# New due times for the planner of a channel-attention and rational-FFN kernel, and a new price for its accumulating transfers

## The chip, the cores and the metric

The kernel runs on one core of a Trainium2 chip. The metric is the device time of one execution in microseconds. The kernel before took 2661.84 us, the median of 3 runs (2660.5 to 2662.58).

## The reference, cut to what matters

There are B = 4 batches of N = 6080 rows with C = 256 channels. Attention runs over channels, so its score matrix is 256 x 256 and each batch needs all of its q and k before the first output row can be made:

```python
qn = q / (norm(q, axis=1) + 1e-6); kn = k / (norm(k, axis=1) + 1e-6)
s = kn.transpose(0, 2, 1) @ qn / tau        # 256 x 256 per batch
a = softmax(s);  x = v @ a                  # 24320 rows of 256
h = x @ w_in                                # 256 -> 2048
P = a0 + a1*h + a2*h*h + a3*h*h*h
Q = 1 + |b0|*|h| + |b1|*h*h
out = (P / (Q + 1e-6)) @ w_out              # 2048 -> 256
```

## The kernel before, in words

**Tiling.** Each batch is cut into 12 groups of 512 rows (the last has 448). The softmax of a batch is folded into w_in (method `fuse`, line 734), so a group is v times eight fused weight tiles and then the rational function. Eight pairs of 128 of the 2048 columns make up a group. In `pair` (line 824) PE writes the pair's h into the two banks of a PSUM tile hx (`mm1`), ACT, DVE and POOL work out P/Q with tiles d, r, uu, gh and gl, and PE multiplies the result by w_out into the one tile acc (`mm2`). There are three hx tiles. `finish_pe` (line 1023) copies acc out by ACT, turns it on PE (the rows acc<-ident,orow), copies it again and stores it. Each pair has one of a few recipes: `KIND` has a four-letter word for each of the eight, and its second letter (F or U here) picks the form of the denominator.

**Attention of the next batch.** `Attn.half` (line 563) runs once for each of the 24 half groups of a batch. It loads k and q (tile kq, four slots), multiplies them on PE (rows hx<-kq, and acc<-kq for the first 12 halves of batch 1, which sum in the acc tile before group 0 gets it), squares them on ACT into one of two sq tiles, and adds the squares to the tile ssq by an accumulating DMA issued from POOL. Each such DMA waits for the one before, since both write ssq. `softmax` (line 621) takes ssq for the norms and then makes the fused weights w.

**The order.** No engine takes its order from the program text. Every operation is handed to `step` with an engine, a cost in us and a due time, and `Planner.order` plays them through once, on the host, while the kernel is built: whenever a modelled engine is free it takes the ready operation with the smallest due time, if its buffers have free slots. A due time is a rank and not a release: an operation due far ahead is taken when nothing due earlier is ready. Some tags hand out their slots in rank order as well. The operations are then emitted in the modelled order, and each engine's queue on the chip is bound to it. So a price that is wrong in the model puts an operation into a queue at a place where the chip must wait. `HOP` is what a result takes in the model to reach another engine; for SP it is 3.5 us, which stands for a transfer.

The due time of a pair's operation is the pair's start, 6.5 us (`II`) a pair, plus `LAG[name][p]`; those of everything else come from `TIME`. Times in `TIME` for attention count in units of 6.5 us from the first group of the batch before (`attn` the pace of the halves, `attn0` where they begin, `attn1` the softmax; `attn_0` and `attn0_0` are the same for batch 1, `front` and `front_pace` for its first 12 halves in us). `start` is where group 0 stands.

**The accumulating transfer in the model.** It is a POOL step of 1.0 us that issues it, followed by an SP step of 0.1 us that runs nothing on the chip and only holds the buffers until the transfer may be taken for landed.

Of the kernel before, what the change touches and what calls it, by code (L numbers as in the profile page):

```python
# [13 lines left out]
AF = mybir.ActivationFunctionType  # L14
ALU = mybir.AluOpType
# [3 lines left out]


LAG = {
    "first": (28.264, 1.351, 30.596, -31.998, 48.265, -7.633, 5.766, 9.407),
    "second": (69.447, 11.924, 13.488, 14.684, 30.047, 41.519, -36.921, -20.262),
    "line": (29.753, 17.275, 56.929, -8.355, -26.962, 38.298, 21.628, 26.132),
    "prod": (-0.029, 21.467, 10.987, 11.927, -9.36, -1.03, 19.608, 29.168),
    "abs": (-26.316, 13.409, 15.158, 16.407, 9.682, 24.255, 8.14, 35.331),
    "one": (96.579, 50.039, 85.796, 127.919, 69.732, 205.132, 99.577, 137.256),
    "slope": (45.923, 29.066, -3.324, 65.5, 12.412, 33.873, 79.042, 20.039),
    "num1": (96.685, 110.5, 60.471, 49.954, 94.518, 84.321, 49.923, 91.338),
    "num2": (2.399, -34.469, -46.621, -37.114, -74.499, -79.273, -83.368, -70.543),  # L30
    "sum": (6.768, -18.247, -28.557, 47.285, -22.402, 24.35, -8.822, -10.898),
    "root": (8.242, 1.503, -31.737, 10.696, -14.224, 31.999, -6.895, -29.514),
    "square": (-59.868, -74.162, -39.607, -12.799, -53.597, -105.617, -43.626, -28.859),
    "quot": (31.717, 37.625, 15.75, 23.688, 20.407, 54.6, 28.307, 47.483),
    "again": (-142.994, -152.496, -145.689, -152.346, -180.413, -123.122, -130.534, -108.094),
    "rest": (-93.002, -56.099, -0.318, -35.317, -0.702, -42.223, -38.726, -56.991),
    "last": (-38.743, -19.238, -20.621, 5.667, -11.108, 14.73, 19.5, -28.157),
    "last_pool": (44.147, 41.875, 61.645, 13.609, 34.415, 42.425, 14.139, -6.356),
    "out": (-5.88, 17.18, 22.743, 26.545, 22.215, 34.239, 21.815, 21.52),
    "out_lo": (90.27, 83.799, 51.937, 68.774, 58.601, 126.426, 69.023, 46.848),  # L40
}
TIME = {
    "pair": 6.5, "start": 100.961, "load": 1.875, "softmax": 71.531, "in": 4.844,
    "late_in": -75.156, "out0": -60.692, "out": 7.965, "attn0_0": -9.298, "attn_0": 1.066,
    "attn0": 72.774, "attn": 0.868, "attn1": 92.735, "value": -3.227, "fuse": 4.772,
    "back": 2.637, "store": -9.728, "finish": -20.927, "front": 41.688, "front_pace": 6.569,
    "ahead_pe": 550004.933, "ahead_act": 339878495500000.0, "ahead_dve": 1357688625.0, "ahead_pool": 12442972510.0,
}


# [231 lines left out]
def tile_channel_attention_rational_ffn(  # L282
# [145 lines left out]
        dve.scalar_tensor_tensor(broot[:, 2:3], broot[:, 2:3], 0.5, broot[:, 1:2], op0=ALU.mult, op1=ALU.mult)  # L428
        dve.tensor_tensor(b1r, broot[:, 0:1], broot[:, 2:3], op=ALU.add)

    if any(kind[1] == "G" for kind in KIND):
        square_root()
    w_in_sb = const.tile([P, NC2, F], F32, name="w_in_sb")
    count = {"R": 0, "S": 0}
# [106 lines left out]
    class Attn:  # L541
# [21 lines left out]
        def half(self, i, at, both, sps):  # L563


            g, half = divmod(i, 2)
            base, pn = groups[g]
            first = self.b == 0
            home = "r" if first and i % 6 >= 3 else "kq"
            kq = buf(home, [P, T // 2, 2, C], F32, "kq")  # L570

            def load():
                for j, src in ((0, k), (1, q)):
                    rows = src[self.b, base : base + pn * T].rearrange("(p t) c -> p t c", t=T)
                    sp.dma_start(kq[:pn, :, j, :], rows[:, half * T // 2 : (half + 1) * T // 2, :])

            step("SP", 1.6, at - (0 if first else 3 if i < self.front else 2 * II), load, self.gate, [kq])

            self.kq[half] = kq
            if first or i < self.front:  # L580
                fn = lambda: self.products(sps, [kq], pn, i == 0, i == (self.front or 2 * NG) - 1)
                step("PE", 1.75, both, fn, [kq, sps] if i else [kq], [sps])
                if i == self.front - 1:
                    fn = lambda: dve.tensor_copy(self.sacc.tile, sps[:, :512])
                    step("DVE", 0.66, both + 1, fn, [sps], [self.sacc])
            elif half == 1:
                pair, slot = list(self.kq), bank("hA")
                step("PE", 3.5, both, lambda: self.products(slot, pair, pn, True, True), pair, [slot])
                if i == 1:
                    fn = lambda: dve.tensor_copy(self.sacc.tile, slot.tile)  # L590
                    step("DVE", 0.66, both + 1, fn, [slot], [self.sacc])
                else:
                    fn = lambda: dve.tensor_tensor(self.sacc.tile, slot.tile, self.sacc.tile, op=ALU.add)
                    step("DVE", 0.66, both + 1, fn, [slot, self.sacc], [self.sacc])
            src = kq, lambda: kq[:pn].rearrange("p t j c -> p (t j c)")
            if i == 0:
                sq = self.ssq = buf("orow" if first else "ssq", [P, 2 * 2 * C], F32)
                step("ACT", 1.05, at, lambda: act.activation(sq[:pn], src[1](), AF.Square), [kq], [sq])
            else:
                sq, total = buf("sq", [P, 2 * 2 * C], F32), self.ssq  # L600
                step("ACT", 1.05, at, lambda: act.activation(sq[:pn], src[1](), AF.Square), [kq], [sq])
                own = first and i % 4 == 3
                e = dve if own else pool
                fn = lambda: e.tensor_tensor(total[:pn], sq[:pn], total[:pn], op=ALU.add)
                if SSQ == "DMA" and not first:
                    begun = Buf()
                    fn = lambda: pool.dma_start(total[:pn], sq[:pn], accum_op=ALU.add)
                    step("POOL", 1.0, at + 2, fn, [sq, total], [begun])
                    step("SP", 0.1, at + 2, lambda: None, [begun, sq, total], [total])
                else:  # L610
                    step(*(("DVE", 1.2) if own else ("POOL", 2.38)), at + 2, fn, [sq, total], [total], True)

# [211 lines left out]
    def pair(m, at, vparts, w, acc):  # L824
# [10 lines left out]
        def c(b):  # L835
            return b[:, :, :n]
# [30 lines left out]
        if kind[1] in "Ff":  # L867
            fn = lambda: act.activation(c(kk), c(hx), AF.Abs, scale=b1)
            put("ACT", 0.87, 0.25, "first", fn, [hx], [kk], 1.0)
            fn = lambda: dve.scalar_tensor_tensor(c(d), c(kk), b0, c(hx), op0=ALU.add, op1=ALU.mult)  # L870
            put("DVE", 1.06, 0.22, "prod", fn, [kk, hx], [d], 1.0)
            fn = lambda: act.activation(c(d), c(d), AF.Abs)
            put("ACT", 0.87, 0.2, "abs", fn, [d], [d])
        elif kind[1] == "G":
            fn = lambda: act.activation(c(d), c(hx), AF.Square, scale=b1r)
            put("ACT", 0.87, 0.25, "first", fn, [hx], [d], 1.0)
            fn = lambda: act.activation(c(kk), c(hx), AF.Abs, scale=b0)
            put("ACT", 0.87, 0.25, "second", fn, [hx], [kk], 1.0)
            fn = lambda: dve.scalar_tensor_tensor(c(d), c(kk), ONE, c(d), op0=ALU.add, op1=ALU.add)
            put("DVE", 1.06, 0.22, "prod", fn, [kk, d], [d], None, True)  # L880
        else:
            fn = lambda: act.activation(c(d), c(hx), AF.Square)
            put("ACT", 0.87, 0.16, "first", fn, [hx], [d], 1.0)
            fn = lambda: act.activation(c(kk), c(hx), AF.Abs, scale=b0)
            put("ACT", 0.87, 0.25, "second", fn, [hx], [kk], 1.0)
            if kind[1] == "A":
                fn = lambda: act.activation(c(d), c(d), AF.Identity, scale=b1, bias=ONE)
                put("ACT", 0.87, 0.27, "line", fn, [d], [d])
            else:
                fn = lambda: pool.tensor_scalar(c(d), c(d), b1, ONE, op0=ALU.mult, op1=ALU.add)  # L890
                put("POOL", 1.06, 0.07, "line", fn, [d], [d])
            fn = lambda: pool.tensor_tensor(c(d), c(d), c(kk), op=ALU.add)
            put("POOL", 2.32, 0.06, "sum", fn, [d, kk], [d])
# [4 lines left out]
        put("DVE", 1.06, 0.16, "num1", fn, [y, hx], [y])  # L898
        fn = lambda: dve.scalar_tensor_tensor(c(hx), c(y), a1, c(hx), op0=ALU.add, op1=ALU.mult)
        put("DVE", 1.06, 0.23, "num2", fn, [y, hx], [hx])  # L900
        fn = lambda: act.activation(c(r), c(d), AF.Abs_reciprocal_sqrt, bias=ONE if kind[1] in "Ff" else 0.0)
        put("ACT", 0.87, 0.2, "root", fn, [d], [r], 6.0)
        if kind[1] == "F":
            fn = lambda: pool.tensor_scalar(c(d), c(d), ones[:, 0:1], ONE, op0=ALU.mult, op1=ALU.add)
            put("POOL", 1.06, 0.07, "one", fn, [d], [d])
        elif kind[1] == "f":
# [212 lines left out]
```

## Time and profile before

| | us |
|---|---|
| median of 3 runs | 2661.84 |
| the profiled execution, its own time | 2666.34 |
| its span, first to last instruction | 2664.3 |
| PE busy | 2555.0 (96%) |
| DVE busy | 2463.1 (92%) |
| POOL busy | 2301.2 (86%) |
| ACT busy | 2235.7 (84%) |

PE is the matmul engine, PEld its weight loads (beside PE), DVE the vector engine, ACT the scalar engine, POOL is GpSimd and SP the engine that issues loads and stores. Nearly every row has line 68, because one helper (`InOrder`) records all operations, so rows are told apart by their tiles: out<-in, without buffer numbers.

### The profile page before, as it was taken

The numbers are of one execution on the slowest core, as the hardware profiler recorded it, in microseconds if no ns is written. First come the engines' busy times: TensorE is split into PE (matmuls) and PEld (weight loads), VectorE is DVE, ScalarE is ACT, GpSimd is POOL, SyncE is SP. The second block draws the span as 40 slices with busy tenths as digits, with TensorE's granted clock in tenths as the row PEclk, the third lists the DMA queues.
The fourth block names the chain that finished last, engine by engine and source line by source line (L and its number), as shares of the span: only waits on it lengthen the run. The fifth ranks groups of instructions, "written<-read, shape, count | busy, mean of one in ns | idle before, by whom it ended". The sixth has DMA issues, their size and how long they took to land.

```text
span 2664.3 us, 30195 instructions
## 1 busy us (share of the span) xinstructions
PE 2555.0 (96%) x9920; PEld 1829.5 (69%) x9920; DVE 2463.1 (92%) x2911; ACT 2235.7 (84%) x2287; POOL 2301.2 (86%) x1773
## 2 busy tenths in 40 slices
PE   7799999999999999999999999999999999999998
PEld 6577766666666666667777666666777766666665
DVE  7689999999979999998888999999787999999997
ACT  5588888888878888988878889888886888888986
POOL 6298999999868999998877999999885899999997
PEclk9899999999999999999999999999999999999999
DMA  9954001001120110105741110101671110110100
GB/s 312 223 131 79 16 16 32 17 15 32 32 55 16 28 21 16 32 16 127 174 91 39 25 24 16 31 18 24 150 172 30 23 25 16 28 21 17 23 9 15
DMA packets 290493, 145.76 MB, mean 55 GB/s; under 512 B 205568, under 2 KB 278528, under 8 KB 290336
## 3 DMA queue, kind: packets, MB, share of 16 engines
q1 hardware_dynamic: 280496, 108.04, 17.2%
q0 software_dynamic: 9840, 35.79, 7.5%
q8 instruction: 78, 1.28, 0.2%
q14 instruction: 79, 0.65, 0.1%
HBM read 83.10 MB, written 24.90 MB: 41 GB/s over the span
## 4 chain that ended last, share of the span: by engine, by line
PE 44%; DVE 27%; ACT 8%; DMA 8%; issue 7%; POOL 5%; SPq 0%; DVEq 0%; POOLq 0%; ACTq 0%
PE hx L68 24%; PE acc L68 20%; DVE d L68 9%; DVE hx L68 8%; DVE uu L68 6%; DMA ssq<-sq 5%; ACT uu L68 4%; POOL d L68 4%; DVE gh L68 2%; ACT r L68 2%; DMA kq<-in_q_dram 2%; DVE orow L68 1%; ACT d L68 1%; POOL gl L68 1%; DMA r<-in_q_dram 1%
## 5 line engine op out<-in xcount | busy, mean ns | idle before, releaser
L68 PE MATMUL hx<-vhi,w 128*128 128x512 f32 (+1 forms) x3072 | 1109.2, 415 | 54.4 <-DVE d L68 37.9
L68 PEld LDWEIGHTS hx<-vhi,w 128*128 128x128 f32 x3072 | 580.9, 189 | 270.9 <-DVE d L68 71.6
L68 PE MATMUL acc<-uu,w_out_sb 128*128 128x512 f32 (+1 forms) x1536 | 690.8, 589 | 1.9 <-DVE uu L68 1.9
L68 PE MATMUL hx<-vlo,w 128*128 128x512 f32 (+1 forms) x1536 | 600.6, 391 | 0.0
L68 POOL TENSOR_TENSOR gl<-d,r 128x512 fp32r<-128x512 f32 (+1 forms) x384 | 497.8, 1312 | 65.5 <-DVE d L68 23.7
L68 POOL TENSOR_TENSOR d<-d,gh 128x512 f32<-128x512 f32 (+1 forms) x384 | 486.2, 1287 | 52.1 <-DVE gh L68 45.2
L68 POOL TENSOR_TENSOR d<-d,r 128x512 f32<-128x512 f32 (+1 forms) x384 | 488.2, 1301 | 31.1 <-ACT r L68 30.2
L68 ACT ACTIVATE uu<-hx,babs 128x1024 f32<-128x1024 f32 (+1 forms) x384 | 422.3, 1100 | 97.6 <-PE hx L68 97.5
L68 DVE SCALAR_TENSOR_TENSOR hx<-uu,coef,hx 128x1024 f32<-128x1024 f32 (+1 forms) x384 | 485.5, 1271 | 2.5
L68 ACT ACTIVATE r<-d 128x1024 f32<-128x1024 f32 (+1 forms) x384 | 401.6, 1047 | 98.9 <-POOL d L68 93.8
L68 PEld LDWEIGHTS acc<-uu,w_out_sb 128*128 128x128 f32 x1536 | 291.2, 190 | 278.9 <-issue 259.3
L68 DVE TENSOR_TENSOR uu<-uu,hx 128x1024 f32<-128x1024 f32 (+1 forms) x384 | 458.7, 1201 | 9.6 <-ACT uu L68 9.5
L68 ACT ACTIVATE uu<-hx,coef 128x1024 f32<-128x1024 f32 (+1 forms) x384 | 457.7, 1192 | 2.8 <-DVE d L68 2.8
L68 ACT ACTIVATE r<-r 128x1024 f32<-128x1024 f32 (+1 forms) x384 | 400.9, 1045 | 5.0
L68 DVE SCALAR_TENSOR_TENSOR d<-uu,babs,hx 128x1024 f32<-128x1024 f32 (+1 forms) x288 | 364.0, 1264 | 33.0 <-ACT uu L68 29.9
L68 POOL TENSOR_SCALAR d<-d,ones 128x1024 f32<-128x1024 f32 (+1 forms) x288 | 326.2, 1135 | 49.5 <-ACT r L68 49.2
L68 ACT ACTIVATE d<-d 128x1024 f32<-128x1024 f32 (+1 forms) x288 | 301.6, 1048 | 70.6 <-DVE d L68 70.2
L68 PEld LDWEIGHTS hx<-vlo,w 128*128 128x128 f32 x1536 | 291.1, 190 | 76.8 <-issue 31.2
L68 DVE SCALAR_TENSOR_TENSOR hx<-hx,coef,r 128x512 f32<-128x512 f32 (+1 forms) x384 | 287.8, 750 | 30.1 <-ACT r L68 23.2
L68 DVE SCALAR_TENSOR_TENSOR d<-hx,coef,d 128x512 f32<-128x512 f32 (+1 forms) x384 | 279.9, 738 | 15.3 <-POOL d L68 15.1
L68 DVE SCALAR_TENSOR_TENSOR gh<-hx,coef,r 128x512 fp32r<-128x512 f32 (+1 forms) x384 | 274.7, 737 | 17.3 <-ACT r L68 10.8
L68 DVE SCALAR_TENSOR_TENSOR uu<-d,hx 128x512 f32<-128x512 f32 (+2 forms) x392 | 261.5, 677 | 20.7 <-POOL d L68 9.2
(99 smaller groups left out, 2893.6 us busy)
## 6 DMA issues: line engine op xcount, KB each, us to landing
ssq<-sq POOLq DMA_DIRECT2D x63, 512.0 KB, 5.7
out_dram<-orow SPq DMA_DIRECT2D x184, 128.0 KB, 2.4
vst<-in_v_dram SPq DMA_DIRECT2D x176, 128.0 KB, 3.8
kq<-in_k_dram SPq DMA_DIRECT2D x78, 256.0 KB, 4.3
kq<-in_q_dram SPq DMA_DIRECT2D x78, 256.0 KB, 5.1
d<-in_moe_w_in_dram SPq DMA_DIRECT2D x8, 512.0 KB, 7.0
ssq<-sq POOLq DMA_DIRECT2D x6, 448.0 KB, 5.4
r<-in_k_dram SPq DMA_DIRECT2D x10, 256.0 KB, 6.5
```

What stands on the lines that cost most here:

```text
L68: ins = op(*args, **kwargs)
```

## The change

Every number of `LAG` and nearly every number of `TIME` is another one. The accumulating transfer's two steps in `Attn.half` get other costs and the SP step another due time. A branch for two new second letters of `KIND`, M and m, is added to `pair`; `KIND` itself is the same.

```diff
-    "first": (28.264, 1.351, 30.596, -31.998, 48.265, -7.633, 5.766, 9.407),
+    "first": (71.3429, 5.5381, 15.3656, 17.3995, 31.0379, -4.663, 41.4562, 27.4064),
-    "slope": (45.923, 29.066, -3.324, 65.5, 12.412, 33.873, 79.042, 20.039),
+    "slope": (-10.955, -25.1691, -21.2353, 3.0526, 3.2465, 29.9361, 19.4443, -40.1467),
-    "out": (-5.88, 17.18, 22.743, 26.545, 22.215, 34.239, 21.815, 21.52),
+    "out": (28.5433, 38.827, 36.0652, 56.0077, -1.6481, 39.3464, 48.688, 25.9075),
...
-    "pair": 6.5, "start": 100.961, "load": 1.875, "softmax": 71.531, "in": 4.844,
-    "late_in": -75.156, "out0": -60.692, "out": 7.965, "attn0_0": -9.298, "attn_0": 1.066,
-    "attn0": 72.774, "attn": 0.868, "attn1": 92.735, "value": -3.227, "fuse": 4.772,
-    "back": 2.637, "store": -9.728, "finish": -20.927, "front": 41.688, "front_pace": 6.569,
+    "pair": 6.5, "start": 119.6723, "load": 1.9885, "softmax": 85.1688, "in": 4.4825,
+    "late_in": -65.9811, "out0": -65.8034, "out": 8.3068, "attn0_0": -2.9056, "attn_0": 1.1935,
+    "attn0": 6.2283, "attn": 1.1347, "attn1": 92.9936, "value": 5.1431, "fuse": 5.8883,
+    "back": 5.3039, "store": -112.0259, "finish": -11.5937, "front": 38.819, "front_pace": 9.8779,
...
-    if any(kind[1] == "G" for kind in KIND):
+    if any(kind[1] in "GMm" for kind in KIND):
...
                     fn = lambda: pool.dma_start(total[:pn], sq[:pn], accum_op=ALU.add)
-                    step("POOL", 1.0, at + 2, fn, [sq, total], [begun])
-                    step("SP", 0.1, at + 2, lambda: None, [begun, sq, total], [total])
+                    step("POOL", 0.95, at + 2, fn, [sq, total], [begun])
+                    step("SP", 2.0, at - 50.0, lambda: None, [begun, sq, total], [total])
...
+        elif kind[1] in "Mm":
...
-        if kind[1] == "F":
+        if kind[1] in "Fm":
```

## Rows read from the trace of the kernel before

**Rows 1.** The page: span, busy time of each engine, and the chain.
```profile
span 2664.3 us, 30195 instructions
...
PE 2555.0 (96%) x9920; PEld 1829.5 (69%) x9920; DVE 2463.1 (92%) x2911; ACT 2235.7 (84%) x2287; POOL 2301.2 (86%) x1773
...
PE 44%; DVE 27%; ACT 8%; DMA 8%; issue 7%; POOL 5%; SPq 0%; DVEq 0%; POOLq 0%; ACTq 0%
...
by line: PE hx L68 24.1%; PE acc L68 19.5%; DVE d L68 8.6%; DVE hx L68 8.4%; issue 6.9%; DVE uu L68 6.4%; DMA ssq<-sq 5.3%; ACT uu L68 4.3%; POOL d L68 3.6%; DVE gh L68 1.9%; ACT r L68 1.6%; DMA kq<-in_q_dram 1.5%; DVE orow L68 1.3%; ACT d 
```

**Rows 2.** Busy time of each engine in ten stretches: us, each engine's, clock, DMA.
```profile
0.00:200.00 200.00, 165.98 (x662) 128.16 (x663) 154.18 (x222) 131.81 (x152) 122.27 (x91) 0.95 0.87 222
200.00:254.70 54.70, 54.70 (x213) 39.39 (x212) 48.99 (x56) 47.15 (x47) 48.80 (x40) 1.00 0.43 76
254.70:694.50 439.80, 431.54 (x1651) 301.37 (x1649) 431.62 (x491) 387.72 (x384) 411.52 (x313) 1.00 0.12 22
694.50:874.40 179.90, 165.30 (x633) 118.37 (x634) 158.70 (x199) 144.93 (x162) 136.98 (x109) 0.96 0.18 38
874.40:1222.80 348.40, 342.25 (x1312) 239.51 (x1311) 341.25 (x390) 306.05 (x302) 327.33 (x248) 1.00 0.12 25
1222.80:1426.70 203.90, 195.32 (x803) 149.20 (x802) 165.29 (x210) 162.25 (x179) 154.00 (x128) 0.98 0.58 128
1426.70:1872.80 446.10, 438.08 (x1679) 307.04 (x1678) 436.50 (x498) 392.29 (x388) 416.07 (x315) 1.00 0.13 25
1872.80:2076.80 204.00, 195.06 (x803) 149.58 (x802) 165.60 (x209) 159.59 (x176) 152.36 (x126) 0.98 0.52 113
2076.80:2616.70 539.90, 530.09 (x2032) 371.08 (x2031) 529.01 (x605) 476.77 (x472) 502.32 (x382) 1.00 0.10 20
2616.70:2664.30 47.60, 36.66 (x145) 25.84 (x143) 31.93 (x42) 27.12 (x31) 29.53 (x27) 0.94 0.09 21
```

**Rows 3.** PE in order of time: start, us, what, idle before and what ended it.
```profile
547.97 1.04 PE L68 MATMUL acc<-ident,orow 128*128 128x128 f32 x8
...
597.60 1.04 PE L68 MATMUL acc<-ident,orow 128*128 128x128 f32 x8
...
972.54 1.04 PE L68 MATMUL acc<-ident,orow 128*128 128x128 f32 x8
...
989.72 0.50 PE L68 MATMUL hx<-vhi,w 128*128 128x512 f32 x1 [0.22 <-DVE uu L68]
...
1020.26 0.50 PE L68 MATMUL hx<-vhi,w 128*128 128x512 f32 x1 [0.85 <-DVE d L68]
...
1021.76 1.03 PE L68 MATMUL acc<-ident,orow 128*128 128x128 f32 x8
```

**Rows 4.** Busy time, in Rows 2's columns, of four single groups.
```profile
972.50:1021.80 49.30, 48.24 (x186) 33.66 (x185) 48.51 (x56) 43.78 (x44) 46.30 (x36) 1.00 0.12 22
254.70:302.70 48.00, 48.00 (x185) 33.58 (x184) 47.16 (x54) 41.94 (x42) 44.25 (x34) 1.00 0.12 23
302.70:350.80 48.10, 46.90 (x179) 32.51 (x178) 47.23 (x54) 43.01 (x43) 44.51 (x35) 1.00 0.11 23
820.30:874.40 54.10, 50.04 (x185) 34.52 (x186) 51.07 (x58) 45.72 (x46) 45.78 (x36) 0.97 0.11 20
```

**Rows 5.** Waits of the whole span: who for whom, us in total, times, longest.
```profile
POOL ssq L68 <- DMA ssq<-sq: 49.8, 23, 8.2
...
PE hx L68 <- DVE d L68: 38.5, 39, 4.3
...
PE hx L68 <- DVE uu L68: 16.2, 36, 3.3
```

**Rows 6.** Waits of the first 200 us, and POOL in order of time there.
```profile
POOL ssq L68 <- DMA ssq<-sq: 31.3, 8, 8.2
...
92.73 0.85 POOL L68 DMA_DIRECT2D ssq<-sq  x1 [7.54 <-DMA ssq<-sq]
101.77 0.85 POOL L68 DMA_DIRECT2D ssq<-sq  x1 [8.20 <-DMA ssq<-sq]
...
116.79 0.86 POOL L68 DMA_DIRECT2D ssq<-sq  x1 [5.72 <-DMA ssq<-sq]
```

**Rows 7.** POOL in order of time at the first change of batch.
```profile
742.16 0.91 POOL L68 DMA_DIRECT2D ssq<-sq  x1 [7.01 <-ACT sq L68]
747.26 0.86 POOL L68 DMA_DIRECT2D ssq<-sq  x1 [4.18 <-DMA ssq<-sq]
755.54 1.12 POOL L68 TENSOR_SCALAR d<-d,babs 128x1024 f32<-128x1024 f32 x1 [7.42 <-ACT d L68]
```

**Rows 8.** POOL's waits from 1180 to 2080 us.
```profile
POOL ssq L68 <- DMA ssq<-sq: 14.3, 14, 2.0
```

**Rows 9.** The page's issues and groups: transfers into ssq, PE's score products.
```profile
ssq<-sq POOLq DMA_DIRECT2D x63, 512.0 KB, 5.7
...
L68 POOL DMA_DIRECT2D ssq<-sq x69 | 63.2, 916 | 80.3 <-DMA ssq<-sq 49.8 <-ACT sq L68 10.3 <-ACT kq L68 8.6
...
L68 PE MATMUL hx<-kq 128*128 128x256 f32 (+1 forms) x576 | 134.3, 387 | 13.5 <-DMA kq<-in_q_dram 8.2 <-DVE uu L68 4.8 <-DVE d L68 0.5
```

**Rows 10.** Tile ssq in the first 260 us: its transfers.
```profile
L68 POOL DMA_DIRECT2D ssq<-sq x23: 828/877/1145, 61.1 to 228.3; - x23
...
DMA to landing us min/median/max: 4.5/5.8/8.5
```

**Rows 11.** PE in order of time after the first change of batch.
```profile
848.48 0.61 PE L68 MATMUL acc<-gl,w_out_hi 128*128 128x512 f32 x2
852.39 0.50 PE L68 MATMUL hx<-vhi,w 128*128 128x512 f32 x1 [3.29 <-DVE uu L68]
```

**Rows 12.** PE in order of time before group 0's first output matmul.
```profile
105.04 3.44 PE L68 MATMUL acc<-kq 128*128 128x256 f32 x8 [2.17 <-DMA kq<-in_q_dram]
...
117.78 1.97 PE L68 MATMUL acc<-kq 128*128 128x256 f32 x8 [0.62 <-DMA kq<-in_q_dram]
...
124.00 1.99 PE L68 MATMUL acc<-kq 128*128 128x256 f32 x8 [0.43 <-DMA kq<-in_q_dram]
...
128.97 0.73 PE L68 MATMUL acc<-gh,w_out_hi 128*128 128x512 f32 x2 [0.21 <-DVE gh L68]
```

More of the change, by code (lines that the diff above doesn't have):

```diff
@@ L21 @@
 LAG = {
-    "first": (28.264, 1.351, 30.596, -31.998, 48.265, -7.633, 5.766, 9.407),
[L23 to L27, printed above, removed]
-    "slope": (45.923, 29.066, -3.324, 65.5, 12.412, 33.873, 79.042, 20.039),
@@ L29 @@
[L29 to L35, printed above, removed]
@@ L36 @@
-    "rest": (-93.002, -56.099, -0.318, -35.317, -0.702, -42.223, -38.726, -56.991),
-    "last": (-38.743, -19.238, -20.621, 5.667, -11.108, 14.73, 19.5, -28.157),
-    "last_pool": (44.147, 41.875, 61.645, 13.609, 34.415, 42.425, 14.139, -6.356),
-    "out": (-5.88, 17.18, 22.743, 26.545, 22.215, 34.239, 21.815, 21.52),
-    "out_lo": (90.27, 83.799, 51.937, 68.774, 58.601, 126.426, 69.023, 46.848),
+    "first": (71.3429, 5.5381, 15.3656, 17.3995, 31.0379, -4.663, 41.4562, 27.4064),
+    "second": (57.6016, 6.8299, -20.0392, 65.122, 96.9876, 47.321, 68.033, 47.1333),
@@ new lines @@
+    "line": (65.7742, 85.1844, 45.4807, 69.7028, 102.0524, 52.2186, 86.2735, 119.3282),
+    "prod": (33.6481, -7.9932, 4.2523, 42.8326, 18.6723, 16.8824, -2.3377, 19.7801),
+    "abs": (-71.6274, -40.8391, -65.9086, -29.463, -32.4482, -52.5393, -46.5113, -29.7792),
+    "one": (118.6179, 105.7, 117.0345, 203.3396, 130.0145, 100.6619, 145.5188, 77.3421),
+    "slope": (-10.955, -25.1691, -21.2353, 3.0526, 3.2465, 29.9361, 19.4443, -40.1467),
+    "num1": (78.6651, 58.3606, 83.6887, 98.6281, 88.3287, 36.9504, 89.5643, 90.0089),
@@ new lines @@
+    "num2": (46.2571, 80.0602, 16.4088, 11.9094, -1.0456, 4.5931, 59.9879, 61.4115),
+    "sum": (123.5526, 77.3211, 81.9855, 64.5573, 78.7551, 62.6624, 184.172, 113.5227),
+    "root": (-28.4521, 11.318, -8.4956, 16.0516, -31.2587, -31.8165, -45.0896, -6.9328),
+    "square": (-14.8172, -36.2736, -35.4794, -76.1768, -62.6297, -97.7208, -140.174, -40.3461),
+    "quot": (55.2294, 25.4683, 30.8856, 87.5384, 92.8464, 97.6642, 90.6668, 50.555),
+    "again": (-156.4485, -135.3792, -114.9349, -150.0496, -110.0526, -129.5206, -172.006, -114.8621),
@@ L41 @@
+    "rest": (3.3676, -65.6467, -68.3869, -44.3422, 10.847, -31.6385, 17.7613, -49.8193),
+    "last": (-31.2746, -86.867, 3.8763, 4.0279, -58.0312, -35.3341, -67.6828, 2.1951),
+    "last_pool": (37.4081, 42.1254, -1.8947, 86.973, 138.0179, 64.0258, 43.4222, 50.4234),
+    "out": (28.5433, 38.827, 36.0652, 56.0077, -1.6481, 39.3464, 48.688, 25.9075),
+    "out_lo": (47.5891, 37.4739, 55.257, 34.8831, 115.3163, 109.322, 93.1246, 39.3377),
 }
 TIME = {
-    "pair": 6.5, "start": 100.961, "load": 1.875, "softmax": 71.531, "in": 4.844,
@@ L44 @@
-    "late_in": -75.156, "out0": -60.692, "out": 7.965, "attn0_0": -9.298, "attn_0": 1.066,
-    "attn0": 72.774, "attn": 0.868, "attn1": 92.735, "value": -3.227, "fuse": 4.772,
-    "back": 2.637, "store": -9.728, "finish": -20.927, "front": 41.688, "front_pace": 6.569,
-    "ahead_pe": 550004.933, "ahead_act": 339878495500000.0, "ahead_dve": 1357688625.0, "ahead_pool": 12442972510.0,
+    "pair": 6.5, "start": 119.6723, "load": 1.9885, "softmax": 85.1688, "in": 4.4825,
+    "late_in": -65.9811, "out0": -65.8034, "out": 8.3068, "attn0_0": -2.9056, "attn_0": 1.1935,
@@ L48 @@
+    "attn0": 6.2283, "attn": 1.1347, "attn1": 92.9936, "value": 5.1431, "fuse": 5.8883,
+    "back": 5.3039, "store": -112.0259, "finish": -11.5937, "front": 38.819, "front_pace": 9.8779,
+    "ahead_pe": 93600.5434, "ahead_act": 7.669400039e+16, "ahead_dve": 15227466580.0, "ahead_pool": 4964001.483,
 }
@@ L873, in pair @@
             put("ACT", 0.87, 0.2, "abs", fn, [d], [d])
+        elif kind[1] in "Mm":
+            fn = lambda: act.activation(c(d), c(hx), AF.Square, scale=b1r)
+            put("ACT", 0.87, 0.25, "first", fn, [hx], [d], 1.0)
+            fn = lambda: act.activation(c(kk), c(hx), AF.Abs, scale=b0)
+            put("ACT", 0.87, 0.25, "second", fn, [hx], [kk], 1.0)
+            if kind[1] == "M":
+                fn = lambda: act.activation(c(d), c(d), AF.Identity, bias=ONE)
+                put("ACT", 0.87, 0.2, "line", fn, [d], [d])
+            begun = Buf()
+            fn = lambda: pool.dma_start(c(d), c(kk), accum_op=ALU.add)
+            put("POOL", 0.0, 0.95, "sum", fn, [d, kk], [begun])
+            step("SP", 2.0, at + LAG["sum"][p] - 50.0, lambda: None, [begun, d, kk], [d])
         elif kind[1] == "G":
@@ L900, in pair @@
         put("DVE", 1.06, 0.23, "num2", fn, [y, hx], [hx])
-        fn = lambda: act.activation(c(r), c(d), AF.Abs_reciprocal_sqrt, bias=ONE if kind[1] in "Ff" else 0.0)
+        fn = lambda: act.activation(c(r), c(d), AF.Abs_reciprocal_sqrt, bias=ONE if kind[1] in "Ffm" else 0.0)
         put("ACT", 0.87, 0.2, "root", fn, [d], [r], 6.0)
-        if kind[1] == "F":
+        if kind[1] in "Fm":
             fn = lambda: pool.tensor_scalar(c(d), c(d), ones[:, 0:1], ONE, op0=ALU.mult, op1=ALU.add)
```

## The prediction

> **What bounds the kernel now.** I read the page's totals first, then cut the span into ten stretches at the points where a group's output is turned on PE (the rows acc<-ident,orow), then the waits of each stretch, and last the single stalls. In the totals PE is busy 2555.0 of 2664.3 us and DVE 2463.1 [rows 1]. The change removes no instruction, so PE's work stays and what can be won is PE's idle time: 2664.3 - 2555.0 = 109.3 us, 4.1%. The ten stretches say where it lies, as length minus PE busy [rows 2]: 34.0 before 200 us, 0 to 254.7, 8.3 to 694.5, 14.6 to 874.4, 6.1 to 1222.8, 8.6 to 1426.7, 8.0 to 1872.8, 8.9 to 2076.8, 9.8 to 2616.7, 10.9 in the tail; together 109.3. Three kinds are to be seen. The front (34.0) waits for loads and for the first softmax. Three short stretches hold a change of batch (14.6, 8.6, 8.9); in the second and third of them the next batch's score products run too. The four long ones are steady groups: 9 + 7 + 9 + 11 = 36 periods with 32.2 us idle, 0.9 each.
>
> One steady period is 1021.76 - 972.54 = 49.22 us from turn to turn [rows 3]. In it PE idles 1.06 us and DVE is busy 48.51 of 49.30; the group from 254.7 does the same matmuls in 48.0 us with PE never idle, beside a DVE that has 47.16 to do there [rows 4]. So in a steady group PE and DVE are both nearly full; the idle microsecond is mostly PE's wait for a bank of hx that DVE still reads, as 0.85 us at 1020.26 [rows 3], and over the run PE's matmuls into hx wait 38.5 us for DVE d and 16.2 for DVE uu [rows 5]. Which instruction is late there is a matter of order, and the order is what changes.
>
> The chain of waits gives 5.3% (141 us) to DMA ssq<-sq [rows 1]. That is not what the transfers cost: the chain follows one thread, while PE is busy through most of these pieces. POOL itself waits 49.8 us for them in 23 waits [rows 5]: 31.3 in the first 200 us [rows 6], 4.2 in the first change of batch [rows 7], 14.3 in the other two [rows 8].
>
> **The change part by part.** (1) What does not run. No entry of KIND has M or m as its second letter (they are F and U), and none has G, so the new branch, the two wider tests and the square root leave the program as it was: 0.
>
> (2) The planner's price of an accumulating transfer. Its POOL part goes from 1.0 to 0.95 (the rows have a mean of 916 ns [rows 9]), and its empty SP step from 0.1 to 2.0 us; with SP's 3.5 us of hand-over the planner now sees the sum of squares free 5.5 us after POOL lets go, where it saw 3.6. The median landing is 5.7 [rows 9], so the plan comes near the chip. The old pace of the later batches, 0.868 x 6.5 = 5.64 us a half, was below one turn of this chain (5.7 and the next issue); the new pace is 1.1347 x 6.5 = 7.38, above it. POOL stalls that stand in the order now because the plan took the data for landed should go. What they are worth to PE is less than their length. In the stretches 1222.8 and 1872.8 PE idles 17.5 us, of which 8 periods at 1.06 would have 8.5 anyway; at most 9.0 us is left, though POOL waited 14.3. From below, the new order could lose there (part 3). I take a gain of 3.
>
> The Trainium skill ("DMA: Bandwidth & Descriptors", section "Anatomy of one DMA — SWDGE (gpsimd) path") fits such a transfer as 2.0 us plus its bytes over 436 kB per us; for 512 KB that gives an estimate of 3.2 us. By that the old 3.6 was right, the new 5.5 spaces the transfers too far, and the 3 here and the 5 of part 3 fall away: 17 becomes 9, still inside the forecast. The trace disagrees: no ssq transfer of the front landed in under 4.5 us and the median is 5.8 [rows 10], so the trace decides.
>
> (3) When attention runs. From the two tables: batch 2 and 3 began their squares and products 72.774 x 6.5 = 473 us after the first group of the batch before and ended at 603, right on the softmax at 92.735 x 6.5 = 603. Now they begin at 6.2283 x 6.5 = 40 and end at 210; the softmax stays at 604. PE's work for it is the same (hx<-kq 134.3 us for 576 matmuls, eight to a half [rows 9], so 45 us for 24 halves), spread over 170 us instead of 130. So the second and third change of batch come to look like the first, whose scores were also ready long before: norms, exponentials and fused weights follow one another with no score products beside them to fill PE. The bound on the bad side is the difference of these stretches: 14.6 - 8.6 and 14.6 - 8.9, 11.7 us in all. Against that stands what made the first one costly: POOL sat 7.01 and 4.18 us before the first two transfers of batch 2, which it took early, and 7.42 more for ACT behind them [rows 7]; the late operations show as PE stalls of 3.29 us a group on [rows 11]. With the landing priced, these need not stand in POOL's order ahead of work that is due. The excess of this stretch over steady groups is 14.6 - 3 x 1.06 = 11.4. I take a gain of 5 in the first change (ends 0 and 11.4), and nothing beyond the 3 above in the others.
>
> (4) The front. All of it is shifted (start 100.961 to 119.6723), which alone moves nothing, because a due time is a rank and not a release. What moves is relative: the twelfth half of batch 1 is due 41.688 + 11 x 6.569 = 113.9, 13.0 after start, and now 38.819 + 11 x 9.8779 = 147.5, 27.8 after start: 14.8 us later against group 0. That matters because these halves sum in the acc tile that group 0 needs for its outputs: the last of them runs at 124.00, and the first output matmul at 128.97 [rows 12]. But the halves are not paced by due times: POOL waits 7.54, 8.20 and 5.72 us for the transfer before [rows 6], one turn of the chain taking about 8 us under the load traffic. So the 14.8 is the far end of a loss; the near end is 0. The far end of a gain is the wait that a later half removes from PE in front of group 0's products: 2.17 + 0.62 + 0.43 us for kq loads [rows 12], 3.2. I take a gain of 3 here, because the batch's remaining halves (due from 194 instead of 124) also stop standing before group 0's work on ACT and POOL.
>
> (5) All other ranks, the steady order. PE's ready matmuls are taken by due time; out moves later in seven of eight pairs, first and slope change places in most, and the finish's copy to the output row goes from -9.728 to -112.0259, that is as soon as it can. No row prices another order of the same operations. Gain: all of 1.06 in 36 periods, 38 us, if every group were as the one at 254.7, but DVE's 48.51 leaves at most 49.22 - 48.51 = 0.7, or 25. Loss: the nearest row of a group out of step is the one from 820.3, no attention in it and 54.10 us long [rows 4], 4.9 more than 49.22, far above anything steady; the worst steady period is 597.60 - 547.97 = 49.63 [rows 3], 0.4 more. I stay near the row that repeats, with a gain of 0.17 a period, 6 us, since the one stall per period that repeats is a matter of order and PE's other waits in the period are under 0.25 us.
>
> Sum: 3 + 5 + 3 + 6 = 17 us. The profiled execution took 2666.3 with 2.0 us around its span, 4.5 above the median 2661.84, so 17 off its own time is 2649, and on the scale of the medians 2661.8 - 17 = 2645.
>
> **The rivals.** *Steady stall grows.* DVE is nearly as full as PE, so an order that puts one long DVE operation wrongly (1.2 us each) ahead of the read that frees a bank makes PE wait longer in every group. The other terms win 11, so this decides from 11 / 36 = 0.3 us a period on: at 49.5 the kernel is as fast as before, at 50.0 it is 0.78 x 36 - 11 = 17 us slower, 2679. For it: 36 repeats of whatever the order does. Against: groups at 48.0 to 48.1 us exist [rows 4].
>
> *Hidden anyway.* The transfers' waits lay beside a full PE, and what the first change wins the other two lose (11.7 against 5 + 3 + 3): 2661, no change.
>
> *The stall closes.* Periods come down by 0.5 us toward DVE's own 48.5: 18 us instead of 6, 2633; with the whole 11.4 of the first change and 9.0 of the others, 2620; with all 25 of the steady groups, 2613.
>
> *It doesn't do what it says.* POOL still waits for transfers as now, because the chip's landing under load (8.5 at most [rows 10]) is longer than the 5.5 planned; the time is then that of the second rival.
>
> **How the numbers follow.** This kernel's runs agree so closely that 0.2%, 5 us, is about what can be told from no change. Forecast (a gain of 6 to 25): 0.42. Stall closes: 0.15. Hidden anyway, with the last rival: 0.13. Steady stall grows: 0.30, since one period counts 36 times and nothing in the trace holds it where it is. Faster 0.57, same 0.13, slower 0.30. The forecast's own range is 2637 to 2656. For 8 in 10 the range goes down to 2613, the far end of the closed stall, and up to 2688, a steady period of 50.25.
>
> **What would show it.** Right: POOL's wait for DMA ssq<-sq falls from 49.8 us to under 20; the DMA bursts move from 1223 and 1873 us to soon after each change of batch; the first change of batch idles PE under 10 us; a steady period is at most 49.1. Wrong: a steady period above 49.5, or second and third changes that idle PE 14 us or more, or a front whose group 0 is turned later than 198.3 us by over 10.

## The result, and the profile after

The changed kernel takes 2624.54 us (median of 4, 2622.15 to 2627.94) against 2662.21 us of the kernel before (4 runs): a ratio of 0.9859 [0.9842, 0.9876], 37.7 us faster. The forecast was 2645 in a range of 2613 to 2688: the sign was right, the size was not; less than half of the gain was foreseen.

The page of the changed kernel, with the lines of [rows 1] and of [rows 9]: span, busy time by engine, chain by engine and by line, and the transfers into ssq.

```profile
span 2626.1 us, 30285 instructions
...
PE 2548.9 (97%) x9920; PEld 1829.2 (70%) x9920; DVE 2452.9 (93%) x2911; ACT 2235.6 (85%) x2287; POOL 2300.1 (88%) x1773
...
PE 54%; DVE 26%; ACT 8%; issue 6%; DMA 4%; SPq 1%; POOL 1%; DVEq 0%; POOLq 0%; ACTq 0%
PE hx L68 29%; PE acc L68 25%; DVE hx L68 8%; DVE d L68 7%; DVE uu L68 6%; ACT uu L68 4%; DVE gh L68 2%; ACT r L68 2%; DMA kq<-in_q_dram 2%; ACT d L68 1%; DMA r<-in_q_dram 1%; SPq L68 1%; DVE orow L68 1%; POOL d L68 0%; ACT orow L68 0%
...
ssq<-sq POOLq DMA_DIRECT2D x63, 512.0 KB, 5.4
```

DMA ssq<-sq has left the chain, every engine runs as many instructions as before, and PE's idle time is 2626.1 - 2548.9 = 77.2 us where it was 109.3. Of the 38.2 us of span, 32.1 are idle time and 6.1 are PE busy time. The waits that answer to [rows 5], and the stretches that answer to [rows 2] (length, then busy us of PE, PEld, DVE, ACT, POOL, then clock, DMA share, GB/s):

```profile
PE hx L68 <- DVE uu L68: 18.5, 18, 3.7
...
PE hx L68 <- DVE d L68: 17.0, 24, 2.1
...
POOL ssq L68 <- DMA ssq<-sq: 14.2, 5, 8.3
```

```profile
0.00:177.10 177.10, 149.40 (x592) 115.24 (x593) 146.44 (x211) 122.46 (x143) 110.21 (x80) 0.95 0.82 212
...
681.10:755.60 74.50, 68.05 (x286) 54.37 (x287) 62.56 (x93) 57.88 (x75) 50.23 (x44) 0.95 0.35 80
755.60:811.30 55.70, 55.34 (x218) 39.70 (x217) 50.94 (x59) 47.85 (x49) 47.49 (x37) 1.00 0.27 62
...
869.70:991.60 121.90, 121.80 (x490) 90.15 (x490) 110.25 (x126) 104.64 (x105) 107.91 (x87) 1.00 0.48 97
...
1324.30:1401.40 77.10, 69.01 (x287) 55.03 (x288) 62.63 (x93) 57.98 (x75) 50.19 (x44) 0.93 0.33 77
...
1970.50:2037.70 67.20, 59.00 (x242) 46.33 (x243) 54.33 (x83) 47.84 (x62) 40.16 (x35) 0.92 0.08 16
...
2092.70:2581.10 488.40, 482.62 (x1836) 334.56 (x1834) 480.07 (x549) 437.10 (x430) 459.54 (x349) 1.00 0.11 21
```

Length minus PE busy is what to read. The row from 869.70 holds attention of batch 2, which now runs there (DMA share 0.48): PE is idle for 0.1 us in 121.9. The three changes of batch idle PE 6.5, 8.1 and 8.2 us; the ten periods from 2092.70 on 5.8, against 9.8 in eleven before. Two turns of the last batch show the steady period, 48.96 us, and its stall, 0.49 where [rows 3] had 0.85. PE in order of time:

```profile
2190.59 1.03 PE L68 MATMUL acc<-ident,orow 128*128 128x128 f32 x8
...
2238.06 0.50 PE L68 MATMUL hx<-vhi,w 128*128 128x512 f32 x1 [0.49 <-DVE d L68]
...
2239.55 0.71 PE L68 MATMUL acc<-ident,orow 128*128 128x128 f32 x5
```

### The profile page after: what moved, and what is told of

The parts are those of the page before. It is cut to its first block, busy times and chain, and to the rows that moved or that the text cites. A ratio compares the mean times of both kernels' runs of the same rounds, so it can differ in the third digit from the quotient of the medians.

```text
span 2626.1 us, 30285 instructions
## 1 busy us (share of the span) xinstructions
PE 2548.9 (97%) x9920; PEld 1829.2 (70%) x9920; DVE 2452.9 (93%) x2911; ACT 2235.6 (85%) x2287; POOL 2300.1 (88%) x1773
## 4 chain that ended last, share of the span: by engine, by line
PE 54%; DVE 26%; ACT 8%; issue 6%; DMA 4%; SPq 1%; POOL 1%; DVEq 0%; POOLq 0%; ACTq 0%
PE hx L68 29%; PE acc L68 25%; DVE hx L68 8%; DVE d L68 7%; DVE uu L68 6%; ACT uu L68 4%; DVE gh L68 2%; ACT r L68 2%; DMA kq<-in_q_dram 2%; ACT d L68 1%; DMA r<-in_q_dram 1%; SPq L68 1%; DVE orow L68 1%; POOL d L68 0%; ACT orow L68 0%
## 5 line engine op out<-in xcount | busy, mean ns | idle before, releaser
L68 PE MATMUL hx<-vhi,w 128*128 128x512 f32 (+1 forms) x3072 | 1087.4, 412 | 37.1 <-DVE uu L68 18.5
L68 ACT ACTIVATE r<-d 128x1024 f32<-128x1024 f32 (+1 forms) x384 | 402.1, 1049 | 20.8 <-POOL d L68 16.3
L68 PE MATMUL acc<-gh,w_out_hi 128*128 128x512 f32 (+1 forms) x768 | 277.8, 443 | 2.8 <-ACT orow L68 1.7
```

Of the source, the lines that this page charges most:

```text
L68: ins = op(*args, **kwargs)
```

## The experiments

Three theories were put up at first. W: the gain is POOL no longer waiting for transfers. P: it is where attention stands. R: it is the ranks of the pair operations. S was their rival: each table fits only its own partner, so that any mixture is slower. The edits are shown shortened. Times are medians; ratios are to the kernel before in the same session (2662 to 2666 us).

### Price and place, one at a time

`price_alone`: the kernel before with the two new `step` lines in `half`.

```diff
-step("POOL", 1.0, ...); step("SP", 0.1, at + 2, ...)
+step("POOL", 0.95, ...); step("SP", 2.0, at - 50.0, ...)
```

> The kernel before with only the planner's price of the accumulating transfer changed (POOL 0.95, SP 2.0 at 50 us earlier); every due time as before. If the gain comes from POOL no longer waiting for transfers (theory W), most of the 38 us is here: 2625 to 2640, with POOL's wait for DMA ssq<-sq down from 49.8 to about 15. If it comes from where attention stands (theory P), under 6 us: 2656 to 2662. If it comes from the ranks of the pair operations (theory R), the same 2656 to 2662, steady period still 49.2. If the tables only work as one set with their price (theory S), slower than before: 2665 to 2690.

2694.6 us, 1.0106 [1.0091, 1.0121].

`tables_alone`: the changed kernel with the old two lines.

> The changed kernel with the old price of the accumulating transfer (POOL 1.0, SP 0.1). W: the gain goes, 2645 to 2662, POOL waits over 40 us for transfers. P and R: nearly all of the gain stays, 2624 to 2632. S: slower than either, above 2650, without POOL's waits explaining it.

2682.7 us, 1.0060 [1.0043, 1.0077]. POOL waits 60.1 us for transfers instead of 14.2:

```profile
POOL ssq L68 <- DMA ssq<-sq: 60.1, 14, 8.0
```

`early_attn_price` and `early_attn_alone`: the kernel before, with and without the new price, and

```diff
-"attn0": 72.774, "attn": 0.868
+"attn0": 6.2283, "attn": 1.1347
```

> The kernel before with the new price and with the attention of batches 2 and 3 at its new place and pace (40 to 210 us after the change of batch instead of 473 to 603); all else as before. P: the stretches with attention beside them run without idle time on PE, so 10 to 15 us are won over the price alone, 2645 to 2652. W: as the price alone. R: no gain beyond the price alone, steady period 49.2. S: slower than before.

> The kernel before, old price, with only the attention of batches 2 and 3 moved to its new place and pace. The fourth corner of the square of price and place. If the price is worth much where attention stands among steady groups, as the loss of 58 us without it in the changed kernel suggests (2682.7 against 2624.5, with POOL waiting 60 us), this is slower than the same with the new price (2671.2): 2690 to 2720, POOL waiting over 50 us. If place and price simply add, it is 2671 - 30 = 2641.

2671.2 us, 1.0027 [1.0017, 1.0037], and 2675.6 us, 1.0039 [1.0029, 1.0050].

`late_attn`: the changed kernel with those two numbers back.

> The changed kernel with the attention of batches 2 and 3 back at its old place and pace (473 to 603 us). P: loses 10 to 15 us, 2635 to 2640, all of it between 680 and 2100 us. W and R: loses under 4 us, 2624 to 2629. S: loses over 20 us, 2645 or more.

2721.5 us, 1.0202 [1.0186, 1.0217].

Every part alone, and the whole without one part, is slower than the kernel before. Price and place do not add: the price costs some 30 us at the old place with the old ranks and wins some 55 in the changed kernel. W, P and R in their plain form, each part carrying its own share, are out. Only S foresaw that every one would lose (`price_alone` by more than it said; `early_attn_alone` lies between its two cases), but the 60.1 us of `tables_alone` speak for W in the changed kernel. Why `price_alone` and `late_attn` lose is not shown: neither was run without its transfers.

### The ranks

`old_lag`: the changed kernel with the old `LAG`. `before_jit1`, `after_jit1`: either kernel with each of the 152 numbers of `LAG` moved.

```diff
-LAG = {k: v}
+LAG = {k: tuple(x + uniform(-2, 2) for x in v)}
```

> The changed kernel, new price and all of its TIME, with the old ranks of the pair operations (LAG). R (the ranks make the gain): 2650 to 2672, close to the 2671.2 of the old kernel with price and place, steady period 49.2. If the front and the other times make it: 2630 to 2640. S (each table fits only its own partner): above 2675.

> The kernel before with each of its 152 pair ranks moved by a random amount within 2 us, nothing else. If due times are worth what they are by their sizes (R), 2 us in ranks that span 350 us does nothing: 2655 to 2675. If one particular order was picked out of many (S), a neighbour has lost the pick: 2680 to 2720, steady period longer than 49.2.

> The changed kernel with each of its 152 pair ranks moved by a random amount within 2 us. R: 2618 to 2632. S: 2640 to 2690; if it then lies where the neighbour of the kernel before lies, the gain of the change belongs to the one order that was found and not to its due times.

2783.9 us, 1.0443 [1.0421, 1.0465]; 2727.0 us, 1.0227 [1.0205, 1.0249]; 2765.1 us, 1.0370 [1.0348, 1.0391]. Ranks that span 350 us cannot be moved by 2: that costs 62 us in one kernel and 140 in the other. Both lie beyond what S had said too. Much of the loss is in the steady groups: in `after_jit1` 31.1 us from turn 4 to 10 and 25.8 in the ten periods from turn 36 (turn n is the first row acc<-ident,orow of group n); the rest is spread over all stretches. Two turns of `after_jit1`, PE in order of time, 50.68 us apart (the next period is 52.1):

```profile
2252.32 1.09 PE L87 MATMUL acc<-ident,orow 128*128 128x128 f32 x8
...
2303.00 1.04 PE L87 MATMUL acc<-ident,orow 128*128 128x128 f32 x8
```

(L87 there is the helper's line, pushed down by the longer tables.) And `late_attn`, whose `LAG` is that of the changed kernel, has last-batch turns 54.56 us apart, with a stall of about 3.45 us in eight groups on end:

```profile
2295.61 1.03 PE L87 MATMUL acc<-ident,orow 128*128 128x128 f32 x8
...
2338.28 0.79 PE L87 MATMUL hx<-vhi,w 128*128 128x512 f32 x1 [3.45 <-DVE uu L87]
...
2350.17 1.03 PE L87 MATMUL acc<-ident,orow 128*128 128x128 f32 x8
```

So the ranks alone do not set the steady period: the same ones give 48.96 and 54.56 us. That it depends on the state in which a stretch is entered is the likely reading, which no run tests. Since planning anew shuffles everything, it cannot tell what one wait costs. The other runs therefore keep a planned order and change what is issued in it.

### The transfers by themselves, in an unchanged order

`before_no_transfer`, `after_no_transfer`: either kernel, the transfer's line issuing nothing.

```diff
-fn = lambda: pool.dma_start(total[:pn], sq[:pn], accum_op=ALU.add)
+fn = lambda: None
```

> The kernel before with the accumulating transfers of batches 1 to 3 left out (69 issues; the norms of these batches then come from one half's squares alone), planned as if they were there, so the order of all else is the same. This is all that transfers can cost the kernel before, issue and wait together. W: 2635 to 2645. Hidden: 2652 to 2664.

> The changed kernel with the same 69 transfers left out. If the change has taken their cost away (W), nothing is left to win: 2618 to 2626. If they cost what they did before, it wins as much as the kernel before does without them.

2626.9 us, 0.9865 [0.9845, 0.9885], and 2617.7 us, 0.9828 [0.9808, 0.9848]. The transfers cost the kernel before 36 us and the changed one 7. The turns of groups 10 and 37 (the same work lies between them in all four) say where. Here they are for the kernel before, for it without transfers, for the changed kernel and for that without transfers, PE in order of time, and then the table made of them:

```profile
694.52 0.87 PE L68 MATMUL acc<-ident,orow 128*128 128x128 f32 x6 [0.32 <-ACT orow L68]
2174.38 0.82 PE L68 MATMUL acc<-ident,orow 128*128 128x128 f32 x6
```

```profile
676.92 0.87 PE L68 MATMUL acc<-ident,orow 128*128 128x128 f32 x6 [0.31 <-ACT orow L68]
2135.19 1.04 PE L68 MATMUL acc<-ident,orow 128*128 128x128 f32 x8
```

```profile
681.09 0.77 PE L68 MATMUL acc<-ident,orow 128*128 128x128 f32 x5
2141.62 0.82 PE L68 MATMUL acc<-ident,orow 128*128 128x128 f32 x6
```

```profile
672.50 0.87 PE L68 MATMUL acc<-ident,orow 128*128 128x128 f32 x6
2132.21 1.04 PE L68 MATMUL acc<-ident,orow 128*128 128x128 f32 x8
```

| us of span | to turn 10 | to turn 37 | to the end | sum |
|---|---|---|---|---|
| before | 694.5 | 1479.9 | 489.9 | 2664.3 |
| before, no transfers | 676.9 | 1458.3 | 490.0 | 2625.2 |
| after | 681.1 | 1460.5 | 484.5 | 2626.1 |
| after, no transfers | 672.5 | 1459.7 | 483.8 | 2616.0 |

Between turns 10 and 37, where the attention of batches 2 and 3 lies, the change wins 19.4 us, all of it transfers (21.6 before, 0.8 after); without them the new order is 1.4 us longer there. Up to turn 10 it wins 13.4, of which 9.0 are transfers (17.6 before, 8.6 after) and 4.4 order. The last stretch, 5.4, is order alone. (These spans are of one profiled execution each; by them the transfers cost 39 and 10.)

`before_stand_in`: each transfer replaced by a POOL memset of 960 columns.

```diff
+fn = lambda: pool.memset(scratch, 0.0)
```

> The kernel before in its planned order with each of the 69 transfers replaced by a POOL memset of a scratch tile of about the issue's length (0.9 us), which waits for the same square but lands at once (the norms are then from one half's squares alone). If POOL's issue time is the price: 2652 to 2664. If the landing is, whoever waits for it: 2625 to 2636.

2628.8 us, 0.9864 [0.9850, 0.9879]. POOL's issue is worth about 2 us, no more than the noise. The memset does not wait for the square, though that was expected of it: POOL is never idle before one, and 9 of the 69 begin before their square is done. So the rest of the 36 us is all that comes with a transfer beside its issue: POOL's wait for the square and for the transfer before, the hold on sq and ssq until the landing, and the transfer's traffic beside the loads. The loads of q do land later beside transfers. The kernel before, and the same without transfers:

```profile
kq<-in_q_dram SPq DMA_DIRECT2D x78, 256.0 KB, 5.1
```

```profile
kq<-in_q_dram SPq DMA_DIRECT2D x78, 256.0 KB, 4.0
```

That is a rival for which no run was made. But the changed kernel moves the same bytes (5.2 us, and 3.8 without transfers), and its transfers cost 0.8 us between turns 10 and 37, so there the traffic alone costs next to nothing; `after_sooner3`, next, moves them too and loses 37. For the front and for the old place the two are not separated.

`after_sooner3`, `before_later2`: the planned order, with each transfer moved in POOL's queue by up to three operations forward or two back, never past a user of its tiles.

> The changed kernel with its planned order kept, but each accumulating transfer up to three POOL operations sooner, so that POOL waits for the one before as it does in the kernel before (45 us or more). W: 2640 to 2665. Hidden: 2624 to 2632.

> The kernel before with its planned order kept on every engine but one: on POOL each accumulating transfer stands up to two POOL operations later, as far as no other user of its sq tile or of ssq is passed; nothing is planned anew. This takes the waits away alone. W (the waits make the gain): 2640 to 2652, POOL's wait for transfers under 25 us. Waits hidden beside a full PE: 2658 to 2670, although the waits are gone.

2661.6 us, 0.9992 [0.9981, 1.0003]: the waits put back into the changed kernel cost it 37 us, all of its gain. POOL now waits 39.4 us for transfers (14.2 before) and 17.7 for squares (4.9):

```profile
POOL ssq L68 <- DMA ssq<-sq: 39.4, 9, 9.1
...
POOL ssq L68 <- ACT sq L68: 17.7, 14, 2.9
```

The other run was a miss: 2754.2 us, 1.0342 [1.0321, 1.0364]. In the kernel before a transfer issued later does not take the wait away: POOL's wait is 52.6 us, and ACT, which needs the transfer's sq tile for the next square, now waits too (19.3 us before). Waits of `before_later2`:

```profile
ACT sq L68 <- DMA ssq<-sq: 94.4, 36, 7.4
...
POOL ssq L68 <- DMA ssq<-sq: 52.6, 13, 7.6
```

### Which hold of the landing costs

`before_two_sums`, `after_two_sums`: odd halves sum in a second tile, so a transfer no longer waits for the one before.

```diff
-fn = lambda: pool.dma_start(total[:pn], sq[:pn], accum_op=ALU.add)
+into = odd_sum if i % 2 else total
+fn = lambda: None if start else pool.dma_start(into[:pn], sq[:pn], accum_op=ALU.add)
...
+dve.tensor_tensor(total.tile, total.tile, odd_sum, op=ALU.add)   # in fold
```

> The kernel before in its planned order, but the squares of odd halves are summed in a second tile, so that each accumulating transfer waits only for the one before the last (22 transfers a batch instead of 23, and one addition more on DVE at the end). If the serial chain is the price (W): 2628 to 2645, close to the 2626.9 without transfers. If the issue on POOL is (0.92 us each): 2655 to 2665.

> The changed kernel with the same two sums. W: 2616 to 2626, as its chain has 7 us left to give (2617.7 without transfers). If the issue is the price: 2624 or more.

2664.7 us, 0.9992 [0.9983, 1.0001], and 2631.0 us, 0.9869 [0.9853, 0.9886]: nothing won, and 6 lost in the changed kernel. W missed both; the times are those foreseen for a price of the issue, but the stand-in has ruled the issue out. The edit is not a clean one: in each of three batches it puts an addition of 1.2 us on DVE right before the softmax.

`before_four_sq`: one sum, but the squares go round four tiles.

```diff
+at_sq = lambda: sq.tile if first or i % 4 < 2 else four[i % 2]
```

> The kernel before in its planned order, one sum, but the squares go round four tiles instead of two, so that ACT's next square does not wait for a transfer to land. If the hold of the sq tiles is the price: 2630 to 2648, ACT's wait for DMA ssq<-sq (19.3 us) gone. If it is the serial chain or the issue: 2658 to 2668.

2664.2 us, 0.9996 [0.9985, 1.0006]. ACT's wait for transfers is gone and nothing is won either. The waits show what stands there instead. Two sums: POOL waits for no transfer, but 39.4 us for squares. Of ACT's own waits before a square, 9.8 us are for a tile still held, and 14.0 for loads (13.3 in the kernel before):

```profile
POOL ssq L68 <- ACT sq L68: 28.7, 8, 9.9
ACT sq L68 <- DMA kq<-in_q_dram: 14.0, 14, 2.2
...
POOL odd_sum L68 <- ACT sq L68: 10.7, 2, 6.6
ACT sq L68 <- DMA odd_sum<-sq: 8.2, 9, 1.8
```

Four tiles: the chain of sums holds POOL as before, 46.4 us in two rows:

```profile
POOL ssq L68 <- DMA ssq<-sq: 30.3, 12, 6.7
...
POOL ssq L68 <- DMA ssq<-four: 16.1, 9, 3.8
```

So neither hold alone is the price. That each stands right behind the other fits these waits but is not shown: both taken away at once was not run, and whether that reaches the 2627 of no transfers is open. The PE stall that is read below stands in both runs as in the kernel before (4.33 and 4.35 us against 4.34).

### Are the neighbours' losses transfers?

`early_attn_no_transfer`, `after_jit1_no_transfer`: the transfers left out as above.

> The kernel before with the new price and place of attention (2671.2) and its transfers left out (norms from one half's squares). If its loss against the kernel before without transfers (2626.9) is still transfers: 2625 to 2640. If it is the old ranks, which put the pair operations badly beside early attention: 2645 to 2665.

> The neighbour of the changed kernel (ranks moved by up to 2 us, 2765.1) without its transfers. If what the neighbour lost is the steady order: 2745 to 2760, steady periods of 51 to 52 as they are. If it is transfers: below 2700.

2663.8 us, 0.9996 [0.9986, 1.0005], and 2751.5 us, 1.0326. At the new place and price the transfers cost 7 us even with the old ranks (2671.2 - 2663.8), as in the changed kernel. But the old ranks there lose 37 us against the same ranks at the old place and price (2663.8 - 2626.9) that have nothing to do with transfers: by the turns, 26 of them lie between 10 and 37 and 10 before turn 10. The neighbour's loss is order too: only 14 of its 140 us go.

## Why the prediction was wrong in size

**What the change is, as the runs show it.** Place and price together take 29 of the transfers' 36 us away. The other new due times, `LAG` and the rest of `TIME`, avoid the 37 us that the old ones lose with that place and price, and win 9 more (2626.9 - 2617.7), in the last batch and the front. So place and price without the new due times were a loss; for the other halves the cause stays open. The forecast's gain was 3 + 5 + 3 + 6 = 17; the spans give 13.4 up to turn 10, 19.4 to turn 37 and 5.4 after it, 38.2.

**Part 2 is the step that failed:** "at most 9.0 us is left ... I take a gain of 3". Between turns 10 and 37 the change took 20.8 us of transfers away (21.6 - 0.8). In the two later changes of batch of the kernel before the transfers cost 252.3 - 241.0 and 252.3 - 240.9, 22.7 us from turn 20 to 24 and from 32 to 36. The ceiling came from PE's idle time less the idle time of as many steady periods, and both halves of that were wrong. Turns 20 to 24 of the kernel before, and of it without transfers (columns as above):

```profile
1222.80:1475.00 252.20, 243.23 (x987) 182.95 (x986) 211.02 (x262) 204.19 (x222) 196.38 (x161) 0.99 0.50 110
```

```profile
1206.40:1447.40 241.00, 238.59 (x988) 181.15 (x987) 208.82 (x262) 203.75 (x222) 176.66 (x138) 1.00 0.25 65
```

PE's idle time falls from 9.0 to 2.4, not to four times 1.06: with score products beside it a group idles less than a steady one (0.6 us here), so less was to be deducted. And PE's busy time falls by 4.6 us for the same matmuls. Where from, the kernel before shows (PE in order of time, and the busy time of the 8 us that follow the stall):

```profile
1372.59 0.74 PE L68 MATMUL hx<-vhi,w 128*128 128x448 f32 x1 [4.34 <-DVE d L68]
1373.13 0.57 PE L68 MATMUL hx<-vlo,w 128*128 128x448 f32 x1
...
1379.74 0.37 PE L68 MATMUL hx<-vlo,w 128*128 128x448 f32 x1
```

```profile
1372.00:1380.00 8.00, 7.41 (x25) 6.72 (x26) 7.04 (x12) 2.04 (x3) 0.00 (x0) 0.59 0.46 75
```

After PE stood for 4.34 us the granted clock is 0.59 of full over these 8 us, mostly the lower of its two levels, and a matmul takes 0.57 us instead of 0.37. Those 0.41 x 8 = 3.3 us, an estimate, were counted as work. In the run without transfers the same matmul waits 0.79 us and the clock stays up:

```profile
1347.48 0.47 PE L68 MATMUL hx<-vhi,w 128*128 128x448 f32 x1 [0.79 <-DVE d L68]
1347.78 0.37 PE L68 MATMUL hx<-vlo,w 128*128 128x448 f32 x1
```

The releaser named there is DVE in both. What holds DVE can be read from two small operations of the softmax, four columns wide. Here they are in the kernel before, with what POOL does beside them, and then both without transfers:

```profile
1368.37 0.94 DVE L68 TENSOR_TENSOR e<-n,e 128x4 f32<-128x4 f32 x1
...
1369.54 1.94 DVE L68 SCALAR_TENSOR_TENSOR e<-y,e 128x4 f32<-128x4 f32 x1
```

```profile
1368.29 1.01 POOL L68 TENSOR_SCALAR d<-d,babs 128x896 f32<-128x896 f32 x1
1369.39 2.07 POOL L68 TENSOR_TENSOR d<-d,uu 128x896 f32<-128x896 f32 x1
```

```profile
1345.80 0.16 DVE L68 TENSOR_TENSOR e<-n,e 128x4 f32<-128x4 f32 x1
...
1346.20 0.16 DVE L68 SCALAR_TENSOR_TENSOR e<-y,e 128x4 f32<-128x4 f32 x1
```

```profile
1346.84 1.01 POOL L68 TENSOR_SCALAR d<-d,babs 128x896 f32<-128x896 f32 x1 [1.09 <-ACT d L68]
```

Each long one ends within 0.03 us of the POOL operation that was running when it began; without transfers POOL still waits for ACT and they take 0.16 us. In these two runs and the changed kernel, every such operation that began beside a running POOL operation was long, and no other was. That is 2.6 of the 3.55 us by which the stall grew. So late transfers cost by moving the engines against each other too: they reach PE through ACT, POOL, DVE and the loads, no wait of PE carries their name, and POOL's 14.3 us [rows 8] were no bound on them either.

**Part 4 failed in the same way.** POOL's 31.3 us in the front were priced by PE's own waits for kq loads, 3.2 us as the far end and 3 as the forecast. Without transfers group 0 is turned at 181.6 instead of 198.3, 16.7 us sooner, and PE's waits for kq loads in front of it [rows 12] are gone. Two ways to this are not told apart: a square that waits for its sq tile keeps its kq slot, so the next load starts late; and the loads themselves land later beside the transfers. The changed kernel turns group 0 at 177.1, gives half of it back to attention that it runs later (turns 0 to 4 take 212.7 instead of 201.7), and keeps 10.2 at turn 4. The feared 14.8 for the later twelfth half did not come.

**Part 3.** The gain in the first change was forecast at 5 and is 14.6 - 6.9 = 7.7 of PE's idle time (turns 10 to 13). The feared loss in the others did not come by that measure: 8.1 and 8.2 idle against 8.6 and 8.9, though no score products of the batch stand beside them any more. But idle time is the measure that failed in part 2, and the clock is 0.93 and 0.92 there. On equal work, without transfers, the new order is 1.4 us longer between turns 10 and 37, so gain and loss of part 3 came to nothing, not to 5.

**Part 5** was right in size where no attention stands: 6 forecast; turns 4 to 10 take 3.2 us less, turns 37 to 46 2.9 and the last group 2.6. That the same order costs 1.4 in between was not seen. Its lower end was wrong. "The worst steady period is 49.63" bounds the runs of one order, not a change of order: ten periods of the last batch average 50.8 us in `before_jit1` and 51.4 in `after_jit1`, past the 50.25 at the far end of the growing stall. And the rival *Hidden anyway* leaves the 6 us of part 5 out of its sum: by its own terms it is 2656, not 2661.

**The Trainium skill's** fit ("DMA: Bandwidth & Descriptors", "Anatomy of one DMA — SWDGE (gpsimd) path") gave an estimate of 3.2 us for a transfer and a sum of 9. The changed kernel's median is 5.4 and its gain 38; the measurement decides against it for these transfers.

**What was foreseen and is so:** POOL's wait under 20 us (14.2), the bursts of DMA soon after each change of batch, the first change under 10 (6.9), a steady period of at most 49.1 (at most 48.97 from turn 37 to 46, but for one of 49.26). None of them measured the price.

## What to carry to other kernels

The idle time of the bounding engine is no ceiling for what a stall elsewhere costs: its busy time holds slow clock too. Leave the suspect out, in the same order, and time that; its waits and its traffic go out with it, so it takes further runs to part them. Where a planner makes the order, correct its prices and find its due times again together, and do not expect a table to survive a small step beside it.

## What was not expected of the hardware

An accumulating transfer of 512 KB from on-chip memory to on-chip memory took 5.4 to 5.7 us to land in the median of the two kernels (4.4 to 9.8 in all). Of the 36 us that 69 of them cost, the issue is about 2: that is what 0.9 us of POOL in the place of each cost. Breaking one of two holds on it, the sum or the tile, won nothing (0.9992 and 0.9996).

A DVE operation of four columns took 0.16 us, and 0.94 to 1.94 when it began beside a running POOL operation, with which it then ended.
